# Row tiles on TensorE, transposes and moves on the DMA queues, and a new order, in a fused attention and feed-forward block

## The chip, the core and the metric

The kernel runs on one core of one Trainium2 chip. Time is device microseconds of one execution, the median of several. The profile is one execution on the same core; its span is a little shorter than the time (204.3 us against 206.0 us for the profiled run).

## What is computed

With S = 2048 tokens, D = 448, 16 heads of 28 and F = 1792, all in bfloat16:

```
xn = (x - mean(x)) / sqrt(var(x) + 1e-5)
q, k, v = split(xn @ wqkv)                  # 448 -> 3 x 448
logits[s, w] = q[s] . k[s - 2 w] / sqrt(28) # w = 0..7, positions below 0 masked
o = softmax(logits) @ v                     # over those 8 positions
s = o @ wo
g = silu(gelu(xn @ w1 + b1) @ w2 + b2)
out = x + s * g
```

## The kernel before

Tokens are reordered when they are loaded: the even positions first, then the odd ones (`tok`, `rows`). The dilated window then becomes eight neighbouring tokens. A query block of 120 tokens (the first has 128, `BLK`) needs 128 keys, so all its scores fit in one 128-key tile, and a 0/1 mask on the exponentials (L515) keeps the eight that count. There are 17 blocks, 16 token tiles of 128 and 4 chunks of 512 tokens.

The stages are: statistics and normalisation of a token tile (L317, L318, L344; the standard deviation is a ScalarE square root, L328); a TensorE transpose of the tile and its copy to SBUF (L352, L356); q and k, made already transposed, 112 rows for 4 heads at a time (L374); v, token by token, in the tiles of keys that the blocks want, so 17 tiles (L414); the first feed-forward matmul with the GELU behind it (L442, L447); the second one with bias, tanh and the product for the SiLU (L462, L475, L479, L483); the attention of a block (L503 to L545); and the output projection with the final sums (L555 to L569). The contraction of 448 is cut into 128 + 128 + 128 + 64; the last tile is padded to 128 with zero rows, so it costs a full matmul. For `w1` one of the padding rows holds `b1`, met by a column of ones in xn.

Four heads share 112 partitions of `kT`, so their scores can't be told apart by one matmul of q. The kernel therefore multiplies q by four 0/1 columns (L389, `hm`) into `qx`, four copies in which only one head's rows are not zero, and one matmul (L503) gives four heads of scores, 480 columns. The attention output of a block is transposed on TensorE (L541) and copied (L545) into `oT` for the projection.

The order of the work is not written by hand. Each stage adds tasks to a `_Plan`: an engine, a planned cost, the tasks it depends on, the buffers it takes and gives, and a priority. `_Plan.run` lays the tasks on the engines one by one, the earliest start first and the priority only between equal starts, and the instructions are emitted in that order. On each engine they then run in exactly this order. PSUM is split by purpose: 3 banks for projections and feed-forward, 2 for scores, 1 for the attention output, 2 for transposes. ScalarE works through one chunk's GELUs, then its exponentials, because each needs another table (`gate`).

Of the kernel before, what the change touches and what calls it, by code (L numbers as in the profile page):

```python
# [13 lines left out]
HOP = 0.10  # L14

# [10 lines left out]
class _Task:  # L26
    __slots__ = ("eng", "cost", "deps", "fn", "prio", "take", "give", "slots",
                 "start", "end", "on", "ndep", "users", "tail", "seq")


class _Plan:
# [7 lines left out]
    def add(self, eng, cost, fn, deps=(), prio=0, take=(), give=(), tail=0.0):  # L39
        t = _Task()  # L40
        t.eng = eng if isinstance(eng, tuple) else (eng,)
        t.cost = cost if isinstance(cost, tuple) else (cost,) * len(t.eng)
        t.deps = [d for d in deps if d is not None]
        t.fn, t.prio, t.take, t.give, t.tail = fn, prio, take, give, tail
        t.slots = {}
        t.start = t.end = None
        t.on = None
        t.users = []
        t.seq = len(self.tasks)
        self.tasks.append(t)  # L50
        for p in take:
            if p.fifo is not None:
                p.fifo.append(t)
        return t

    def run(self):
# [4 lines left out]
        free = {}  # L61
        ready = [t for t in self.tasks if not t.ndep]
        order = []
        while ready:
            best = None
            for t in ready:
                slot_at = 0.0
                ok = True
                for p in t.take:
                    if not p.free or p.fifo and p.fifo[0] is not t:  # L70
                        ok = False
                        break
                    slot_at = max(slot_at, min(p.free)[0] + HOP)
                if not ok:
                    continue
                for e, c in zip(t.eng, t.cost):
                    at = max(free.get(e, 0.0), slot_at)
                    for d in t.deps:
                        at = max(at, d.end + (0.03 if d.on == e else HOP))
                    key = (round(max(at, free.get(e, 0.0)), 2) + (c if len(t.eng) > 1 else 0.0) * 0.5,  # L80
                           -t.prio, t.seq)
                    if best is None or key < best[0]:
                        best = (key, t, e, c, at)
            if best is None:
                raise RuntimeError("the plan is stuck: " + str([(t.seq, t.eng, t.fn.__qualname__) for t in ready[:20]]))
            _, t, e, c, at = best
            t.on, t.start = e, at
            free[e] = at + c
            t.end = at + c + t.tail
            for p in t.take:  # L90
                s = min(p.free)
                p.free.remove(s)
                t.slots[id(p)] = s[1]
                if p.fifo is not None:
                    p.fifo.pop(0)
            for p, owner in t.give:
                p.free.append((t.end, owner.slots[id(p)]))
# [11 lines left out]
    def emit(self):  # L109
        done = set()  # L110
        for t in self.order:
# [3 lines left out]
            t.fn(t)  # L115
# [3 lines left out]
def kernel(  # L119
# [12 lines left out]
    nc = tc.nc  # L132
# [6 lines left out]
    KT = 4  # L139
    NMT = F // P  # L140
# [4 lines left out]
    GW = 4 * DH  # L145
# [3 lines left out]
    BLK = [(0, 128, 0)] + [(128 + 120 * i, 120, 120 + 120 * i) for i in range(16)]  # L149
    NB = len(BLK)  # L150
# [17 lines left out]

    x_sb = sb("x_sb", [P, NT, D])
    wqkv = sb("wqkv", [P, KT, 3 * D])  # L170
    w1 = sb("w1", [P, KT, F])
    w2 = sb("w2", [P, NMT, D])
    wo = sb("wo", [P, G, D])
    b2 = sb("b2", [P, D])
    xnT = [sb(f"xnT{c}", [P, KT, CH]) for c in range(NCH)]
    qx = [[sb(f"qx{g}_{c}", [P, 4, CH]) for c in range(2)] for g in range(G)]
    kT = [sb(f"kT{g}", [P, S]) for g in range(G)]
    oT = sb("oT", [P, G, S])
    g2 = [sb(f"g2_{t}", [P, D]) for t in range(NT)]
    ident = sb("ident", [P, P])  # L180
    eps_t = sb("eps_t", [P, 1], F32)
    hm = sb("hm", [P, 4], F32)
    m_gen = sb("m_gen", [P, 4, 120])
    m_b0 = sb("m_b0", [P, 4, 128])
    m_sp = sb("m_sp", [P, 4, 120])
# [7 lines left out]
    p_xn = ring("xn", 3, [P, 512])  # L193
    p_st = ring("st", 4, [P, 6], F32)
    p_q = ring("q", 3, [P, CH])
    p_E = ring("E", 4, [P, 4, P], fifo=True)
    p_rd = ring("rd", 2, [P, H], F32)
    p_os = ring("os", 2, [P, D])
    p_y = ring("y", 2, [P, D], F32)
    p_t = ring("t", 2, [P, D], F32)  # L200
    p_sg = ring("sg", 2, [P, D])
    p_h = ring("h", 19, [P, CH], fifo=True)
    p_v = ring("v", 9, [P, H, 32], fifo=True)
    p_o = ring("o", 3, [P, D])

    def bank(name, shape, dt=F32):
        return psum.tile(shape, dt, name=name)

    p_mm = _Pool([bank(f"mm{i}", [P, 512]) for i in range(3)])
    p_sc = _Pool([bank(f"sc{i}", [P, 4, P]) for i in range(2)], True)  # L210
    p_po = _Pool([bank("po0", [P, H, 32])], True)
    p_tp = _Pool([bank(f"tp{i}", [P, 4, P], BF16) for i in range(2)])
# [3 lines left out]
    def buf(pool, owner):  # L216
        return pool.bufs[owner.slots[id(pool)]]
# [4 lines left out]
    def act(n):  # L222
        return 0.19 + n / 1200.0

    def dve(n, r=1):
        return 0.15 + n / (960.0 * r)

# [6 lines left out]
    POOLC, DVEC = "POOL", "DVE"  # L234
    t_eps = plan.add(DVEC, 0.1, memset("vector", eps_t[:], EPS), prio=99)
    t_pad = []
    for xb in p_xn.bufs:
        a = plan.add(DVEC, 0.1, memset("vector", xb[:, 448:], 0.0), prio=98)
        t_pad.append(plan.add(DVEC, 0.1, memset("vector", xb[:, 448:449], 1.0), [a], prio=98))
# [5 lines left out]
    t_ident = plan.add(POOLC, 0.6, mk_ident, prio=99)  # L245
    t_wz = plan.add(POOLC, 1.2, memset("gpsimd", wqkv[64:, 3, :], 0.0), prio=98)
    t_w1z = plan.add(POOLC, 1.8, memset("gpsimd", w1[64:, 3, :], 0.0), prio=97)

    def mk_hm(_):
        nc.gpsimd.memset(hm[:], 1.0)  # L250
        nc.gpsimd.affine_select(out=hm[:], in_=hm[:], compare_op=ALU.is_ge, fill=0.0, base=0,
                                pattern=[[-DH, 4]], channel_multiplier=1)
        nc.gpsimd.affine_select(out=hm[:], in_=hm[:], compare_op=ALU.is_ge, fill=0.0, base=DH - 1,
                                pattern=[[DH, 4]], channel_multiplier=-1)
    t_hm = plan.add(POOLC, 0.6, mk_hm, prio=96)

    def mk_masks(_):
        for m, n, lo, hi in ((m_gen, 120, -1, 8), (m_b0, 128, 7, 0)):
            nc.gpsimd.memset(m[:], 1.0)
            nc.gpsimd.affine_select(out=m[:], in_=m[:], compare_op=ALU.is_ge, fill=0.0, base=lo,  # L260
                                    pattern=[[0, 4], [-1, n]], channel_multiplier=1)
            nc.gpsimd.affine_select(out=m[:], in_=m[:], compare_op=ALU.is_ge, fill=0.0, base=hi,
                                    pattern=[[0, 4], [1, n]], channel_multiplier=-1)
        q0, n, k0 = BLK[SPLIT]
        j = HALF - q0
        nc.gpsimd.tensor_copy(m_sp[:], m_gen[:])
        nc.gpsimd.affine_select(out=m_sp[:, :, j:], in_=m_sp[:, :, j:], compare_op=ALU.is_ge,
                                fill=0.0, base=k0 - HALF, pattern=[[0, 4], [0, n - j]],
                                channel_multiplier=1)
    t_vw = [plan.add(POOLC, 0.5, memset("gpsimd", v[:], 1.0), prio=80 - i) for i, v in enumerate(p_v.bufs)]  # L270
    t_E = [plan.add(POOLC, 0.5, memset("gpsimd", e[:], 0.0), prio=90) for e in p_E.bufs]
    t_mask = plan.add(POOLC, 5.0, mk_masks, prio=85)

    dma_at = [2.0]

    def dma(eng, dst, src, kb, deps=(), prio=50, give=()):
        def fn(_):
            (nc.sync if eng == "SP" else nc.scalar).dma_start(dst(), src)
        return plan.add(eng, 0.6, fn, deps, prio, give=give, tail=2.0 + kb / 230.0)

    xr = x_sb
    t_x = {}

    def load_x(t0, n, eng, prio, kb):
        d = dma(eng, lambda: xr[:, t0:t0 + n, :],
                rows(x_half, t0 * P, n * P).rearrange("(t p) d -> p t d", p=P), kb, prio=prio)
        for t in range(t0, t0 + n):
            t_x[t] = d

    load_x(0, 1, "SP", 99, 112)  # L290
    load_x(1, 1, "SP", 98, 224)
    load_x(2, 2, "SP", 97, 448)
    t_wqk = [dma("ACT", lambda: wqkv[:, 0:3, 0:2 * D],
                 A_wqkv[0:384, 0:2 * D].rearrange("(k p) c -> p k c", p=P), 900, prio=99),
             dma("ACT", lambda: wqkv[:64, 3, 0:2 * D], A_wqkv[384:448, 0:2 * D], 1000, prio=98),
             t_wz]
    t_wv = [dma("ACT", lambda: wqkv[:, 0:3, 2 * D:],
                A_wqkv[0:384, 2 * D:].rearrange("(k p) c -> p k c", p=P), 1400, prio=97),
            dma("ACT", lambda: wqkv[:64, 3, 2 * D:], A_wqkv[384:448, 2 * D:], 1400, prio=96), t_wz]
    load_x(4, 4, "SP", 96, 1600)  # L300
    load_x(8, 4, "SP", 95, 2000)
    load_x(12, 4, "SP", 94, 2400)
    t_w1 = [dma("SP", lambda: w1[:, 0:3, :], B_w1[0:384, :].rearrange("(k p) c -> p k c", p=P), 3000, prio=93),
# [329 lines left out]
```

The softmax here doesn't subtract the row's maximum and nothing guards it: scores larger than these inputs give would overflow.

## Time and profile before

| | |
|---|---|
| time, median of 3 | 206.07 us (206.0 to 206.94) |
| span of the profiled execution | 204.3 us |
| busy: PE, PEld, DVE, ACT, POOL | 179.2, 96.2, 117.0, 117.2, 14.6 us |
| first projection matmul starts | 12.89 us |
| last output-projection matmuls end | 200.7 us |
| weights, x and outputs moved | 8.80 MB |

PE is TensorE, PEld its weight loads, DVE is VectorE, ACT is ScalarE, POOL is GpSimd, SP is the queue that issues most transfers. The busy time of one matmul is longer than its distance to the next one, because matmuls overlap in the array: the rows of the groups give the first, the chain of work that ended last gives the second. An engine's idle time counts only where the chain passes through it.

### The profile page before, as it was taken

The numbers are of one execution on the slowest core, as the hardware profiler recorded it, in microseconds if no ns is written. First come the engines' busy times: TensorE is split into PE (matmuls) and PEld (weight loads), VectorE is DVE, ScalarE is ACT, GpSimd is POOL, SyncE is SP. The second block draws the span as 40 slices with busy tenths as digits, with TensorE's granted clock in tenths as the row PEclk, the third lists the DMA queues.
The fourth block names the chain that finished last, engine by engine and source line by source line (L and its number), as shares of the span: only waits on it lengthen the run. The fifth ranks groups of instructions, "written<-read, shape, count | busy, mean of one in ns | idle before, by whom it ended". The sixth has DMA issues, their size and how long they took to land.

```text
span 204.3 us, 3123 instructions
## 1 busy us (share of the span) xinstructions
PE 179.2 (88%) x1192; PEld 96.2 (47%) x1192; DVE 117.0 (57%) x330; ACT 117.2 (57%) x204; POOL 14.6 (7%) x32
## 2 busy tenths in 40 slices
PE   0269849989999999989999999899999999799952
PEld 0146324445555644545556544455565544365530
DVE  2795980037987930069977800279976400289992
ACT  0316735786554587766535687855545786856610
POOL 8991000000000000000000000000000000000000
PEclk9999988999999999999999999999999999999995
DMA  6999100000000000000000000000100000000010
GB/s 195 359 369 362 42 0 3 0 0 0 5 22 22 26 0 0 0 0 3 30 16 26 22 0 0 0 3 0 50 22 22 0 0 3 0 0 26 24 45 23
DMA packets 8320, 8.80 MB, mean 43 GB/s; under 512 B 497, under 2 KB 7857, under 8 KB 8306
## 3 DMA queue, kind: packets, MB, share of 16 engines
q1 hardware_dynamic: 7346, 7.40, 11.0%
q10 hardware_dynamic: 960, 1.20, 1.8%
q8 instruction: 9, 0.15, 0.3%
q14 instruction: 5, 0.04, 0.1%
HBM read 6.77 MB, written 1.84 MB: 42 GB/s over the span
## 4 chain that ended last, share of the span: by engine, by line
PE 76%; DVE 13%; ACT 6%; DMA 2%; issue 1%; ACTq 0%; DVEq 0%
PE mm L442 25%; PE mm L462 18%; PE mm L374 13%; PE mm L555 6%; PE sc L503 6%; PE mm L414 4%; PE po L522 3%; DVE st L317 2%; ACT L509 2%; DMA wqkv<-in_A_wqkv_dram 2%; DVE qx L389 2%; DVE E L515 2%; PE tp L541 1%; ACT E L509 1%; DVE xnT L356 1%
## 5 line engine op out<-in xcount | busy, mean ns | idle before, releaser
L442 PE MATMUL mm<-xnT,w 128*128 128x512 bf16 x224 | 51.0, 388 | 0.0
L509 ACT ACTIVATE E<-sc 128x480 bf16<-128x480 f32 (+1 forms) x68 | 36.0, 570 | 23.5 <-PE sc L503 23.2
L462 PE MATMUL mm<-w,h 128*128 128x448 bf16 x224 | 47.6, 352 | 0.0
L447 ACT ACTIVATE h<-mm 128x512 bf16<-128x512 f32 x56 | 32.8, 597 | 13.6 <-PE mm L442 13.1
L442 PEld LDWEIGHTS <-w 128*128 128x128 bf16 x224 | 22.2, 100 | 27.7 <-issue 2.9
L515 DVE TENSOR_TENSOR E<-E,m_gen 128x480 bf16<-128x480 bf16 x60 | 23.1, 402 | 19.1 <-ACT E L509 18.1
L374 PE MATMUL mm<-xnT,wqkv 128*112 128x512 bf16 x128 | 30.4, 391 | 1.0 <-DVE xnT L356 1.0
L462 PEld LDWEIGHTS <-h 128*128 128x128 bf16 x224 | 21.2, 97 | 18.3
L356 DVE COPY xnT<-tp 128x512 bf16<-128x512 bf16 x16 | 6.5, 419 | 38.5 <-PE tp L352 38.5
L374 PEld LDWEIGHTS <-wqkv 128*112 128x112 bf16 x128 | 17.0, 135 | 11.9 <-issue 2.2
L503 PE MATMUL sc<-qx,kT 112*128 112x480 bf16 (+4 forms) x80 | 22.4, 334 | 0.0
L389 DVE TENSOR_SCALAR qx<-q,hm 112x512 bf16<-112x512 bf16 x64 | 18.0, 348 | 6.7 <-ACT q L364 6.7
L522 PE MATMUL po<-v,E 128*128 128x29 bf16 x272 | 17.1, 177 | 4.1 <-DVE E L515 3.9
L522 PEld LDWEIGHTS <-E 128*128 128x128 bf16 x272 | 14.0, 96 | 13.3 <-DVE E L515 8.0
L352 PE MATMUL tp<-ident,xn 128*128 128x128 bf16 x64 | 6.4, 241 | 13.9 <-DVE xn L344 13.9
L555 PE MATMUL mm<-wo,oT 112*128 112x448 bf16 x64 | 15.1, 358 | 0.9 <-DVE oT L545 0.9
L364 ACT CAST q<-mm 112x512 bf16<-112x512 f32 x16 | 9.4, 585 | 10.1 <-PE mm L374 9.5
L479 ACT ACTIVATE t<-y 128x448 f32<-128x448 f32 x16 | 9.2, 577 | 8.8 <-DVE y L475 8.8
L364 ACT CAST kT<-mm 112x512 bf16<-112x512 f32 x16 | 9.4, 586 | 7.2 <-PE mm L374 7.2
L475 DVE TENSOR_TENSOR y<-mm,b 128x448 f32<-128x448 f32 x16 | 10.0, 623 | 3.5 <-PE mm L462 3.5
L352 PEld LDWEIGHTS <-xn 128*128 128x128 bf16 x64 | 4.5, 106 | 15.7 <-DVE xn L344 15.0
L364 ACT CAST v<-mm 128x448 bf16<-128x448 f32 x17 | 9.1, 533 | 5.0 <-PE mm L414 5.0
(49 smaller groups left out, 146.3 us busy)
## 6 DMA issues: line engine op xcount, KB each, us to landing
out_dram<-o SPq DMA_DIRECT2D x16, 112.0 KB, 1.7
w<-in_B_w_dram SPq DMA_DIRECT2D x1, 1568.0 KB, 11.0
x_sb<-in_A_x_dram SPq DMA_DIRECT2D x3, 448.0 KB, 7.9
w<-in_B_w_dram SPq DMA_DIRECT2D x1, 1344.0 KB, 9.5
wqkv<-in_A_wqkv_dram ACTq DMA_DIRECT2D x1, 672.0 KB, 4.4
wo<-in_A_wo_dram SPq DMA_DIRECT2D x1, 392.0 KB, 7.8
wqkv<-in_A_wqkv_dram ACTq DMA_DIRECT2D x1, 336.0 KB, 6.5
x_sb<-in_A_x_dram SPq DMA_DIRECT2D x2, 112.0 KB, 3.6
```

The source lines that it names most:

```text
L352: nc.tensor.transpose(tp[:, kt, :], xn[:, kt * P:(kt + 1) * P], ident[:])
L364: nc.scalar.copy(o, i)
L374: nc.tensor.matmul(ps[:GW, :], wqkv[:, kt, which * D + GW * g:which * D + GW * (g + 1)], xnT[c][:, kt, :], start=(kt == 0), stop=(kt == KT ...
L389: nc.vector.tensor_scalar(qx[g][c % 2][:GW, hl, :], q[:GW, :], hm[:GW, hl:hl + 1], None, op0=ALU.mult)
L442: nc.tensor.matmul(ps[:, :], w1[:, kt, mt * P:(mt + 1) * P], xnT[c][:, kt, :], start=(kt == 0), stop=(kt == KT - 1))
L447: nc.scalar.activation(buf(p_h, _)[:], buf(p_mm, a)[:, :], ACT.Gelu_apprx_tanh)
L462: nc.tensor.matmul(ps[:, :D], buf(p_h, t_h[(c, mt)])[:, j * P:(j + 1) * P], w2[:, mt, :], start=(mt == 0), stop=(mt == NMT - 1))
L503: nc.tensor.matmul(ps[:, :, lo - q0:hi - q0], kT[g][:GW, k0:k0 + P], qx[g][c % 2][:GW, :, lo - c * CH:hi - c * CH], start=True, stop=True)
L509: nc.scalar.activation(buf(p_E, k)[:, :, :nq], buf(p_sc, a)[:, :, :nq], ACT.Exp, scale=SCALE)
L515: nc.vector.tensor_tensor(out=E[:, :, :nq], in0=E[:, :, :nq], in1=m[:, :, :nq], op=ALU.mult)
L522: nc.tensor.matmul(ps[:, h, :DH + 1], E[:, hl, :], buf(p_v, t_v[b])[:, h, :DH + 1], start=True, stop=True)
L555: nc.tensor.matmul(ps[:, :D], oT[:GW, g, t * P:(t + 1) * P], wo[:GW, g, :], start=(g == 0), stop=(g == G - 1))
```

## The change

The change keeps the arithmetic and moves it. Its parts:

- **32-row tiles for the scores.** q and k are now made token by token (`qk_rows`), evacuated with each head padded from 28 to 32 columns, and transposed by DMA into `qkT`, so that a head lies in a 32-partition strip. Sixteen small matmuls of 120 columns make a block's scores, each using 32 rows of the array; four of them, in different strips, write four different banks. The four masked copies of q are no longer needed.
- **64-row pairs for the tails.** The 64-row remainder of the contraction is no longer padded. It lies at partitions 0 to 63 in one half of the tiles and at 64 to 127 in the other, and two tails, one from each half, are issued one after the other (`batch`). Bias `b1` moves into the GELU instruction.
- **DMA instead of engines.** From tile 4 on, xn is transposed by a DMA on the SP queue (`dma_T`), and so are q, k and the attention output. v is computed once per token tile (16 instead of 17) and moved by GpSimd-issued DMAs (`dma_sb`) to the key tiles; the attention output is moved in the same way from blocks of 120 to tiles of 128.
- **The deviation on GpSimd.** (var + eps) to the power -0.5 replaces the square root on ScalarE and a reciprocal on VectorE.
- **Loads in order of use.** x and wqkv come first, in slices by contraction tile, and the first projections follow the slices (`first_batch`); w2 is held back until half of w1 is there, and half of x and wo until later (`hold`). Matmuls on zeros run on TensorE before the data come.
- **One pool of 8 PSUM banks** for everything, and a planner that knows tables, array modes and priorities taken from a list (`PRIO`, `LATER`). The last token tile is worked in two halves of 224 columns. The order of the work is: GELU 0, attention 0 and 1 with the projections of all the later chunks, GELU 1, attention 2, GELU 2, attention 3, GELU 3, each followed by its second feed-forward matmuls.

The core of the diff, with the lines that matter:

```diff
-    p_mm = _Pool([bank(f"mm{i}", [P, 512]) for i in range(3)])
-    p_sc = _Pool([bank(f"sc{i}", [P, 4, P]) for i in range(2)], True)
-    p_po = _Pool([bank("po0", [P, H, 32])], True)
-    p_tp = _Pool([bank(f"tp{i}", [P, 4, P], BF16) for i in range(2)])
+    p_b = _Pool([psum.tile([P, 512], F32, name=f"bank{i}") for i in range(8)])
...
+    def dma_sb(dst, src, deps, prio, take=(), give=()):
+        def fn(k):
+            nc.gpsimd.dma_start(dst(k), src())
...
+    def dma_T(dst, src, deps, prio, give, n=1):
+        def fn(_):
+            nc.sync.dma_start_transpose(out=dst, in_=src())
...
-            nc.scalar.activation(sd[:, t0:t0 + n], mv[:, t0:t0 + n, 1], ACT.Sqrt, bias=eps_t[:])
-            nc.vector.reciprocal(rstd[:, t0:t0 + n], sd[:, t0:t0 + n])
+            nc.gpsimd.tensor_scalar(sd[:, t0:t0 + n], mv[:, t0:t0 + n, 1], eps_t[:], None, op0=ALU.add)
+            nc.gpsimd.tensor_tensor(out=rstd[:, t0:t0 + n], in0=sd[:, t0:t0 + n], in1=half_t[:, :n], op=ALU.pow)
...
+        if t >= TPC:
+            t_xT[t] = dma_T(xnT[:, :, t * P:(t + 1) * P], lambda: buf(p_xn, a)[:], [a], PRIO["turn_x"][t], (p_xn, a, 0))
+            return
...
+    def batch(close, opened, prio):
...
+            todo = [[(j, i) for i, j in enumerate(every) if j.half == h] for h in range(2)]
+            while todo[0] or todo[1]:
+                for h in range(2):
+                    if todo[h]:
+                        j, i = todo[h].pop(0)
...
+        def tail(ps, start, stop):
+            nc.tensor.matmul(ps[:], w1[r, 3, ms], xnT[r, 3, cs], start=start, stop=stop)
...
-                    nc.tensor.matmul(ps[:, :, lo - q0:hi - q0], kT[g][:GW, k0:k0 + P],
-                                     qx[g][c % 2][:GW, :, lo - c * CH:hi - c * CH], start=True, stop=True)
+            for g in range(G):
+                for hl in range(4):
+                    r = slice(32 * hl, 32 * hl + 32)
+                    nc.tensor.matmul(buf(p_b, k, hl)[:, g * nq:(g + 1) * nq], qkT[r, 1, g, k0:k0 + P],
+                                     qkT[r, 0, g, q0:q0 + nq], start=True, stop=True)
...
-                nc.tensor.transpose(tp[:GW, g, :nq], os_[:nq, GW * g:GW * (g + 1)], ident[:nq, :nq])
-            nc.vector.tensor_copy(oT[:GW, :, q0:q0 + nq], buf(p_tp, tr)[:GW, :, :nq])
+            first, d = dma_sb(lambda k, t=t, row=row, n=n: buf(p_ot, ot_at.get(t, k))[row:row + n, :D],
+                          lambda q=q, n=n: buf(p_os, o)[q - q0:q - q0 + n, :], [o] + t_os + mine + [d for _, d in ot[t]],
+                t_oT[t] = dma_T(oT[:, :, t * P:(t + 1) * P], lambda t=t: buf(p_ot, ot_at[t])[:], [d for _, d in ot[t]], PRIO["turn_o"][t],
+                                (p_ot, ot_at[t], 0))
...
+    for c, what in ((0, "F"), (0, "A"), (1, "A"), (1, "F"), (2, "A"), (2, "F"), (3, "A"), (3, "F")):
```

How many instructions of each kind the two kernels hold, on the engines that the change moves:

| | before | after |
|---|---|---|
| first feed-forward, 512 columns | 224 full | 168 full, 56 of 64 rows |
| q and k | 128 of 512 columns | 96 of 448, 32 of 64 rows and 448 |
| v, 448 columns | 68 full | 48 full, 16 of 64 rows |
| scores | 80 (480 columns in most) | 272 of 32 rows and 120 columns |
| attention times v, 29 columns | 272 | 272 |
| transposes on TensorE | 132 | 16 |
| DMA transposes on SP | 0 | 45 |
| GpSimd-issued DMAs | 0 | 67 |
| ScalarE table loads | 9 | 8 |
| changes of the array's tile size in TensorE's order | 0 | 72 |

## The prediction

> **What bounds the kernel now.** I read the shares of busy time and the 40 slices first, to see whether one engine is busy throughout.
>
> ```profile
> PE 179.2 (88%) x1192; PEld 96.2 (47%) x1192; DVE 117.0 (57%) x330; ACT 117.2 (57%) x204; POOL 14.6 (7%) x32
> ...
> PE   0269849989999999989999999899999999799952
> PEld 0146324445555644545556544455565544365530
> DVE  2795980037987930069977800279976400289992
> ```
>
> PE is full from the fourth slice to the last but two, with holes at the start, near slices 5 and 6, and at the end. VectorE comes in bursts of up to 9 tenths, so it is close behind PE in the attention stages. The chain that ended last says the same: 76% of the span on PE.
>
> ```profile
> PE 76%; DVE 13%; ACT 6%; DMA 2%; issue 1%; ACTq 0%; DVEq 0%
> ```
>
> So time is won by taking columns off PE, or by closing holes. To price PE I need the distance between matmuls, not their busy time (388 ns for 512 columns holds some of the neighbour's time too). The chain in order of time gives it:
>
> ```profile
> 73.48 12.25 PE mm L442 x56
> ...
> 68.41 4.32 PE mm L374 x20
> ...
> 95.67 0.21 PE sc L503
> ...
> 95.89 0.76 PE mm L555 x4
> ...
> 96.84 1.33 PE mm L462 x7
> 98.17 0.21 PE tp L541 x4
> 98.38 0.09 PE po L522 x4
> ```
>
> A matmul of 512 columns takes 12.25/56 = 0.218 us (L374: 0.216), one of 448 columns 1.33/7 = 0.190, four transposes 0.21, a score matmul 0.21, four small matmuls of 29 columns with their four weight loads 0.09.
>
> Before, PE's sum is then: L442 224 x 0.218 = 48.8; L462 32 x 1.33 = 42.6; L374 128 x 0.216 = 27.6; L414 68 x 0.190 = 12.9; L555 16 x 0.77 = 12.3; scores 68 x 0.21 = 14.3; L522 68 x 0.09 = 6.1; transposes of x and of the attention output 33 x 0.21 = 6.9. Together 171.5. The first projection starts at 12.89 and the last matmuls end at 200.7, which is 187.8 us; so some 16 us in between are holes, 12.9 is the start and 3.6 the tail. The windows show the first hole and the end:
>
> ```profile
> 25.00:29.00 4.00, 0.48 (x6) 0.36 (x7) 3.84 (x14) 1.06 (x3) 0.00 (x0) 1.00 0.00 0
> 29.00:43.00 14.00, 14.00 (x65) 6.23 (x64) 1.10 (x6) 8.85 (x15) 0.00 (x0) 0.88 0.00 1
> ...
> 174.00:200.70 26.70, 22.93 (x201) 12.66 (x199) 20.20 (x51) 14.21 (x26) 0.00 (x0) 0.98 0.06 18
> ```
>
> Columns: length, then busy time of PE, PEld, DVE, ACT, POOL, then granted clock. From 25 to 29 us PE waits while VectorE does statistics (3.5 us lost), and after it the clock is 0.88 for 14 us (1.6 lost). In the last 27 us PE loses nearly 4, because the last attention blocks run through VectorE with no other matmuls left to fill in.
>
> **What the Trainium skill says.** TensorEngine Tiling (Array Packing), Key Properties: tiles of the array work independently and in parallel, and changing the tile size drains the array. No run so far shows either; what the trace gives is the pipeline that a drain would empty, 388 - 218 = 170 ns. TensorE: Matmul & The Clock Gate, Measured speedup vs the span model: four 32-row tiles with 512 columns ran 3.07 times faster than one by one; not shown here. DMA: Bandwidth & Descriptors, Latency and other measured facts: a DMA has some 2 us of fixed cost, and a transposing one moved 261 GB/s; the trace agrees with the first (112 KB stores land 1.7 us after issue) and has no transpose. SBUF - State Buffer, the "DVE blocks DMA" trap: GpSimd can't write the descriptors of its own DMAs while VectorE runs a two-port operation; no such DMA is in this trace.
>
> **The change on PE.** Tails in pairs: 168 full matmuls and 28 pairs in place of 224, (168 + 28) x 0.218 = 42.7, 6.1 less than before. Second feed-forward matmul: unchanged, 42.6. q and k: (96 + 16) x 0.190 = 21.3, 6.3 less. v: (48 + 8) x 0.190 = 10.6, 2.3 less. Output projection 12.3 and attention times v 6.1, unchanged. Transposes: two of the four that remain come after the first projection, 0.4; 6.5 less. All this counts a pair as one matmul.
>
> Scores: 16 small matmuls in a block. If four stream side by side, 120/512 of 0.218 x 16/4 = 0.20 us; one by one 0.82; the nearest row is L522, where 16 small matmuls with 16 weight loads take 4 x 0.09 = 0.36. I take 0.37, as the weight loads are of the same width: 17 x 0.37 = 6.3, 8.0 less than before. (Ends: 3.4 and 13.9.)
>
> Added: 72 changes of tile size, 19 groups of tails and 17 of scores, each entered and left. One costs between 0 and the 0.17 us of the pipeline; I take the middle, 0.085: 6.1. (Ends: 0 and 12.2.)
>
> PE's sum after: 42.7 + 42.6 + 21.3 + 10.6 + 12.3 + 6.1 + 0.4 + 6.3 + 6.1 = 148.4, 23 less than before.
>
> **The start.** Before, the first matmul waits for all four tiles of the chunk, for a table load behind ACT's own transfers (to 6.98) and the order of VectorE's work. After, tile 0 alone starts it: its statistics end at 4.3 in the trace, then two tiny GpSimd operations (0.11 to 0.2 each in the rows of small GpSimd work; 0.5 with the hops), xn 0.47 and its tail's copy (0.15), transposes and copy about 1.1: 6.6 us. The wqkv slices (1.2 MB behind 0.45 MB of x, at the 360 GB/s of the early slices) are there by 4.6 + 2. So 6.3 us come off. The first half of w1 follows by about 10 us, before it is wanted at about 15 (6.6 + 42 x 0.19), and statistics of later tiles run under the first GELUs, when VectorE had almost nothing to do: the hole at 25 us and the slow clock behind it should go.
>
> **Holes.** Of the 16 us before, 5 go with that hole, and about 4 at the end, since the last attention blocks now come ahead of the last GELUs; 7 stay. New waits: a block's scores want four banks at once, freed by four exponentials of 0.57 in a row, with the next blocks of PE's order queued behind them; q and k pass a DMA (2 + 0.26 MB/261 GB/s = 3.0 us by the page's prices) before the scores, the attention output two of them (about 2 + 2.5) before the projection. PE's order has other matmuls between, so most of it is hidden; I add 3, with 0 and 15 as ends.
>
> **The other engines.** ScalarE: exponentials 38.7, GELUs 33.4, tanh 9.4, 34 copies of 0.53 (18.1), 8 tables of 1.28: 110. VectorE: masks 27.3, statistics 12.5, y, g and sg 30, normalised outputs and reciprocals 14.7, xn 8.6, 15 evacuations 9.3, o and the rest 8: 111. Both stay under 148. The tightest place is between the first and the second group of GELUs: by the new order PE has about 34 us there, ScalarE 32 exponentials, 4 tanh, 17 copies and a table, 31, and VectorE 8 blocks of 2.5, 4 tiles of y and g (5.0), statistics of 4 tiles (3.1), xn of 8 (4.2) and 5 evacuations (3.1), 35, part of which can slip under the next GELUs. Removed from VectorE are L389 (18.0), L356 and L545 (10) but evacuations and late statistics come into the same stretch; this is why I leave 3 us of new holes and not 0. SP: 45 transposes and 17 stores; at 3.0, 2.5 and 1.7 us with no overlap at all 16 x 3.0 + 28 x 2.5 + 17 x 1.7 = 147. GpSimd: 61 moves of about 1 us, off the path. Both are hidden if those prices hold.
>
> **Sum.** Start 6.6 + PE 148.4 + holes 10 + tail 3.4 (half-size last pieces) = 168.4; the time lies 1.7 above the span before, so 170. I give 169, since the drains and the score loads may partly overlap.
>
> **Rivals.** (a) Tiles don't run side by side and every drain costs the full pipeline. Then tails cost 28 x 0.218 + 24 x 0.190 = 10.7 more, scores 17 x 0.45 = 7.6, drains 6.1: 193, still faster. For it: nothing in the trace shows two matmuls in parallel. Against: L522 takes 23 ns for each pair of load and matmul, so issue is no obstacle. (b) A wait takes the place of columns: banks, or q, k and attention output coming late out of their DMA, 3 to 4 us in each of four attention stages, about 14: 183. For it: the chain of a block gets two or three DMA trips longer, and the tight stretch above. Against: the blocks of other chunks lie between. (c) The queue becomes the bound: if each transpose holds SP for twice the price, one after the other, 16 x 6 + 28 x 5 + 29 = 265 us of queue, and even with a third of it overlapped the end is at about 215, slower than before. For it: all 45 stand in one queue, in a fixed order, each holding up those behind it. Against: a fixed cost that is mostly latency overlaps with the next transfer, as the stores' and loads' do here.
>
> **Chances.** 68% for the sum (160 to 178), 9% for (a), 16% for (b), 6% for (c), 1% for no change. Faster by more than 0.5%: 0.93; same 0.01; slower 0.06. The range must hold the sum and (b), and leaves (a) and (c) out: low end with free drains, 0.2 us of scores and no new holes (169 - 6 - 3 - 3, and a little for pairs), 158; high end 184.
>
> **What would show it.** In the profile after: pairs of tails 0.22 us apart in the chain, not 0.44; a block's 16 scores in about 0.4 us; first L498 matmul near 6.6 us; no PE hole at 25 us, clock near 1 from the start; PE's share of the chain above 85%; SP transposes landing in 2 to 4 us. I am wrong if the waits of PE name DMA tiles (qkT, oT, v) or banks for more than 10 us in all, if tails don't pair, or if transposes queue behind each other.

## The result and the profile after

The median of four runs is 171.19 us (170.53 to 172.78), against 206.07 us (206.0 to 206.94) for the kernel before in the same runs: a ratio of 0.831, 95% interval 0.823 to 0.839. Here and below, an execution over 1.5% above the fastest one of its kernel counts as slow and is left out of times and ratios, though the traces of tails_one_half and plain_priorities are of such executions. The forecast was 169 us in a range of 158 to 184. The profiled execution took 172.78 us, the longest of the four; its span is 171.1 us, 33.2 less than before.

The page of the kernel after gives busy time, the slices that answer to those shown of before, and the granted clock. A slice is 4.3 us here.

```profile
PE 156.6 (92%) x1313; PEld 77.4 (45%) x1313; DVE 101.9 (60%) x271; ACT 102.7 (60%) x183; POOL 52.1 (30%) x114
...
PE   7999999904999999999999999999999999999950
PEld 2644344402454564334445454335555545445640
DVE  4778530039489988965047888004988994605770
...
PEclk9999999975599999999999999999999999999998
```

PE is full nearly from the second slice to the end, except for one hole in slices 9 and 10, and the clock drops to 0.5 behind it. The chain that ended last has only 72% on PE and 15% on transfers:

```profile
PE 72%; DMA 15%; issue 3%; DVE 3%; POOL 3%; SPq 0%; DVEq 0%; POOLq 0%
```

Some pieces of this chain in order of time give the distances between matmuls (start, length, count):

```profile
98.47 0.32 PE bank L636 x16
98.80 0.20 PE bank L658 x4
...
138.60 2.59 PE bank L557 x12
141.19 0.97 PE bank L560 x8
142.16 2.70 PE bank L557 x12
144.86 0.79 PE bank L658 x32
...
148.46 1.43 PE bank L593 x7
```

L557 is a full matmul of 512 columns, still 2.59/12 = 0.216 us. L560 are eight tails of 64 rows: 0.97 us is four times 0.218 and 0.10 for the change of tile size, so two tails cost as much as one full matmul. The group behind them takes 2.70 in place of 2.59, which is the change back, 0.11. A block's scores (L636) take 0.32 us in the chain; with the same 0.10 for the change, 0.22 are left for the columns. The four small matmuls of L658 behind them take 0.20 in place of 0.09, again the change back.

The windows of the kernel after, in the columns of the prediction's windows, cut the span where PE's state changes:

```profile
7.66:34.10 26.44, 26.33 (x174) 11.72 (x172) 11.61 (x35) 16.68 (x28) 11.48 (x21) 1.00 1.08 229
34.10:40.80 6.70, 0.01 (x2) 0.01 (x1) 3.80 (x11) 0.71 (x2) 1.62 (x4) 0.69 0.66 207
40.80:48.00 7.20, 7.20 (x39) 3.07 (x39) 4.69 (x12) 4.02 (x9) 1.48 (x2) 0.57 0.29 57
48.00:164.10 116.10, 116.10 (x1060) 58.67 (x1059) 75.45 (x185) 79.62 (x144) 30.72 (x56) 1.00 0.52 95
```

So the span is: start 7.66, first stretch 26.4, a hole of 6.7, a stretch of 7.2 at 0.57 of the clock (3.1 lost), 116 us in which PE never waits, and a tail of 7.0. PE's own work is 164.07 - 7.66 - 6.7 - 3.1 = 146.6 us, against the 171.5 summed up for before.

What made the hole stands in the waits from 12 to 41 us of the same trace:

```profile
DVE st L391 <- DMA x_sb<-in_A_x_dram: 14.3, 2, 13.6
...
PE bank L658 <- DVE E L650: 6.7, 1, 6.7
...
POOL x_sb L739 <- DMA xnT<-xn: 3.9, 1, 3.9
```

PE waited for the masked exponentials of the first block, but they were late only because VectorE, which works in a fixed order, had stood for 13.6 us on the statistics of tile 8. Its x had not been asked for: GpSimd issued that load at 32.14, after `hold` (L739) had waited for the transposed tile 7. And tile 7 stood in the SP queue behind the transposes of q and k, which the timeline of SP shows (start, length, engine, line, operation):

```profile
13.82 15.05 SPq L351 DMA_TRANSPOSE qkT<-qk_tok  x4
28.96 15.59 SPq L351 DMA_TRANSPOSE xnT<-xn  x5
```

Four transposes took 15 us to issue, while w2 (1568 KB) was moving from 13.66 to 26.8; most later ones took 1.2 to 1.3 us each. That the load is what slowed them isn't shown by a run of its own. Tile 7 is the first of the five x transposes, issued at 28.96, and the hold could run at 31.59.

### The profile page after: what moved, and what is told of

The parts are those of the page before. It is cut to its first block, busy times and chain, and to the rows that moved or that the text cites. A ratio compares the mean times of both kernels' runs of the same rounds, so it can differ in the third digit from the quotient of the medians.

```text
span 171.1 us, 3569 instructions
## 1 busy us (share of the span) xinstructions
PE 156.6 (92%) x1313; PEld 77.4 (45%) x1313; DVE 101.9 (60%) x271; ACT 102.7 (60%) x183; POOL 52.1 (30%) x114
## 4 chain that ended last, share of the span: by engine, by line
PE 72%; DMA 15%; issue 3%; DVE 3%; POOL 3%; SPq 0%; DVEq 0%; POOLq 0%
PE bank L593 22%; PE bank L557 16%; DMA w<-in_B_w_dram 12%; PE bank L498 10%; PE bank L700 7%; PE bank L658 4%; PE bank L524 4%; PE bank L560 3%; PE bank L636 3%; DMA x_sb<-in_A_x_dram 3%; PE bank L501 2%; DVE st L391 1%; PE bank L527 1%; DVE y L609 1%; DVE sg L705 0%
## 5 line engine op out<-in xcount | busy, mean ns | idle before, releaser
L593 PE MATMUL bank<-w,h 128*128 128x448 bf16 (+1 forms) x238 | 46.5, 342 | 0.0
L564 ACT ACTIVATE h<-bank,b 128x512 bf16<-128x512 f32 x56 | 34.2, 692 | 12.5 <-PE bank L560 6.5
L557 PE MATMUL bank<-xnT,w 128*128 128x512 bf16 x168 | 39.1, 379 | 0.0
L642 ACT ACTIVATE E<-bank 128x480 bf16<-128x480 f32 (+1 forms) x68 | 33.3, 581 | 9.6 <-PE bank L636 9.4
L345 POOL DMA_DIRECT2D ot<-os x31 | 16.8, 545 | 52.7 <-DVE os L670 38.1
L345 POOL DMA_DIRECT2D v<-v_tok x30 | 16.3, 549 | 29.2 <-ACT v_tok L303 18.0
L557 PEld LDWEIGHTS <-w 128*128 128x128 bf16 x168 | 15.5, 98 | 20.7 <-issue 3.8
L498 PE MATMUL bank<-w_in,xnT 128*128 128x448 bf16 x96 | 24.5, 380 | 0.1
L658 PEld LDWEIGHTS <-E 128*128 128x128 bf16 x272 | 11.3, 97 | 13.1 <-DVE E L650 7.1
L700 PE MATMUL bank<-wo,oT 128*128 128x448 bf16 (+1 forms) x68 | 14.7, 341 | 0.0
L524 PE MATMUL bank<-w_in,xnT 128*128 128x448 bf16 x48 | 12.1, 352 | 0.0
L670 DVE TENSOR_TENSOR os<-bank,rd 120x448 bf16<-120x448 f32 (+1 forms) x17 | 10.6, 622 | 0.5
L658 PE MATMUL bank<-v,E 128*128 128x29 bf16 x240 | 10.7, 176 | 0.0
```

The lines of the kernel that those rows point to most:

```text
L345: nc.gpsimd.dma_start(dst(k), src())
L498: nc.tensor.matmul(ps[:, :D], xnT[:, kt, cs], w_in[:, kt, which * D:(which + 1) * D], start=start, stop=stop)
L524: nc.tensor.matmul(ps[:, :D], xnT[:, kt, k0:k0 + P], w_in[:, kt, 2 * D:], start=start, stop=stop)
L557: nc.tensor.matmul(ps[:], w1[:, kt, ms], xnT[:, kt, cs], start=start, stop=stop)
L564: nc.scalar.activation(buf(p_h, own, i)[:], buf(p_b, own, i)[:], ACT.Gelu_apprx_tanh, bias=b1[:, mt:mt + 1])
L593: nc.tensor.matmul(ps[:, :n], buf(*h_at[(c, mt)])[:, j * P:(j + 1) * P], w2[:, mt, cs], start=(mt == 0), stop=(mt == NMT - 1))
```

## Experiments

Each ratio is to runs of the kernel before taken with it; in microseconds of that kernel, 0.01 is 2.1 us. All but two kernels are edits of the kernel after (171.19 us, 0.831). The first five try the theory of the hole and the two kinds of tiles.

**x_early** issues the load of x 8 to 15 right behind w2 and b2, without the hold. `move` takes tasks out of the finished order and puts them behind another.

```diff
     load_x(12, 4, 85, "POOL", [t_hold])
+    held = t_hold
...
     plan.run()
...
+    issues = [t_x[8].deps[0], t_x[12].deps[0]]
+    held.fn = None
+    for t in issues:
+        t.deps = []
+    move(issues, t_b2.deps[0])
```

> The changed kernel with one edit: the loads of x tiles 8 to 15 are issued right behind w2 and b2 and no longer wait for the last turned tile of chunk 1; all other orders stay. Mine: the hole of 6.7 us on TensorE at 34 us is a queue on VectorE, statistics of tile 8 that wait for this load ahead of the first masks. x then lands near 31 in place of 36.8 us, the hole shrinks to under 2 us, the clock stays at 1, and the time falls by 5 to 8 us, to about 164. Rival: the DMA engines are simply full until 40 us, so the earlier load pushes w2 and the turned tiles back by as much and the hole only moves: within 1.5 us of 171.

Measured: 164.13 us, ratio 0.794 (0.789 to 0.799), as I expected. The clock is 0.99 and PE's largest hole 1.4 us, a wait for a transposed tile of x:

```profile
PE bank L498 <- DMA xnT<-xn: 1.4, 1, 1.4
```

It follows that the held load was the cause: the hole of 6.7 us and the slow clock went. The only other thing that moved is the load of wo, which stood behind the same hold and goes out at 26.20 in place of 33.69 us; its first user, L700, runs long after the hole.

**stats_later** leaves the load as it is and moves VectorE's statistics of tiles 8 to 11 behind the masks and sums of the first block.

```diff
+    dve = [t for t in plan.order if t.on == "DVE"]
+    xn8 = next(t for t in dve[dve.index(t_st[11]):] if t.fn.__qualname__.endswith("norm.<locals>.f1"))
+    move([t_st[t] for t in range(8, 12)] + [t_rs[8]], dve[dve.index(xn8) - 1])
```

> The changed kernel with one edit: on VectorE the statistics of tiles 8 to 11 stand behind the first block's masks and the first y and g, not ahead of them; loads are untouched. Mine: the masks run at 33 us, attention times v follows at once and the hole of 6.7 us at 34 us goes by at least half, though xn of tile 8 still waits for its x and holds up the masks of the second block; 3 to 6 us less. Rival: TensorE waits for loads whatever VectorE's order, so the hole stays and the time is within 1.5 us of 171.

Measured: 169.26 us, 0.818 (0.814 to 0.823), 1.9 us less and not the 3 to 6 that I expected. The old wait went, and a new one of 4.2 us came later on PE, with a slow clock behind it:

```profile
PE bank L636 <- DVE os L670: 4.2, 1, 4.2
```

The scores wait here for a bank that VectorE frees only after the statistics and xn of tile 8, which still begin at 36.60 us, when x has landed. So VectorE's order hands the wait on, but most of the late load still has to be paid.

**tails_one_half** puts all first feed-forward tails into the lower half of the array, with the order untouched.

```diff
-        r = slice(64 * half, 64 * half + 64)
+        r = slice(0, 64)
```

> The changed kernel with one edit: all 56 tails of the first feed-forward matmul use partitions 0 to 63, so no two of them can lie side by side; same order, same number of instructions. Mine: pairs do run side by side, so 28 pairs of 0.218 us become 56 in a row: 6.1 us slower, 177. Rival: tails run one after the other already, each with its own columns: no change.

Measured: 175.08 us, 0.848 (0.844 to 0.853). In the chain, eight tails take twice the columns:

```profile
143.89 1.83 PE bank L560 x8
```

1.83 - 0.97 = 0.86, or 0.215 for each of the four tails that no longer find a partner. All 28 pairs make 6.0 us on PE. Of this 4.2 us show between the spans (175.3 and 171.1 us) and 3.9 between the medians: chunk 0's seven pairs, 1.5 us, fall ahead of the hole, which is 1.2 us shorter in this trace (5.5 us). The pairs do run side by side.

**scores_by_strip** makes the scores strip after strip, so that neighbours in PE's order share a strip.

```diff
-            for g in range(G):
-                for hl in range(4):
+            for hl in range(4):
+                for g in range(G):
```

> The changed kernel with one edit: a block's 16 score matmuls are issued strip by strip (four in one 32-row strip, then the next strip) and not strip after strip in turn. Mine: overlap needs neighbours in different strips, so most of the side-by-side work is lost: a block's scores take 0.6 to 0.8 us in place of 0.22 and the 17 blocks 6 to 10 us more, near 179. Rival: matmuls of other strips overtake, and the time stays at 171 with scores at 0.2 us.

Measured: 173.34 us, 0.840 (0.837 to 0.844), an interval that overlaps that of the kernel after. A block's scores take 0.35 us in place of 0.32:

```profile
48.70 0.35 PE bank L636 x16
```

In this trace the hole is 8.1 us long, 1.4 more, so the 2.1 us between the medians can't be put down to the scores. My expectation was wrong and the rival's right about the size: neighbours in the same strip cost next to nothing. That a matmul waiting for its strip lets those of other strips pass is one explanation, and no run shows it. It was left open whether strips matter at all:

**scores_one_strip** takes every head's q and k from the first strip, so the scores of the other heads are replaced by those of the first in each group of four.

```diff
-                    r = slice(32 * hl, 32 * hl + 32)
+                    r = slice(0, 32)
```

> The changed kernel with one edit: all 16 score matmuls of a block read the first 32-row strip, so the three other heads of each group get the first one's scores; the output is not the reference's. Instructions, columns and order are the same. Mine: here nothing can lie side by side, so a block's scores take 16 x 120 columns at 2.4 a ns, 0.8 us in place of 0.22 to 0.32, and 17 blocks 8 to 10 us more, near 180; the run by strips was quick because matmuls of the next strip start while the last is still streaming. Rival: a small matmul costs its issue of about 14 ns whatever its strip, and the side-by-side tiles gained nothing: 171 to 173.

Measured: 181.68 us, 0.876 (0.868 to 0.885), 10.5 us more by the medians. The chain has every block at

```profile
48.16 0.94 PE bank L636 x16
```

Without the change of tile size this is 0.84 against 0.22, a factor of 3.8 for four strips; 17 blocks times 0.62 us are 10.5. So strips run side by side.

**x8_early** follows from x_early, whose two loads shared the DMA engines with w2: only tiles 8 to 11 go early, 12 to 15 stay held.

```diff
-    t_hold = hold(x_sb[:1, 8:NT, 0], xnT[:1, 0, 8 * P - 1:8 * P].to_broadcast((1, 8)), [t_xT[7]], 180)
+    t_hold = hold(x_sb[:1, 12:NT, 0], xnT[:1, 0, 8 * P - 1:8 * P].to_broadcast((1, 4)), [t_xT[7]], 180)
...
+    issues = [t_x[8].deps[0]]
+    for t in issues:
+        t.deps = []
+    move(issues, t_b2.deps[0])
```

> The changed kernel with x tiles 8 to 11 alone loaded behind w2; tiles 12 to 15 stay held as in the changed kernel. x_early kept a hole of 1.4 us at 34 us, where TensorE waits for the turned tile 4, which stands behind four transposes that share the DMA engines with w2 and 0.9 MB of x. Mine: with 0.45 MB less in that stretch the turned tile lands 1 us or more sooner and the hole goes: about 163. Rival: the queue of transposes sets it and the time is x_early's, 164.

Measured: 162.92 us, 0.787 (0.783 to 0.790), the fastest version, 8.3 us below the change as it was made. The interval just touches x_early's, so the times hardly tell these two apart; the traces do. The page of x8_early shows no hole at all:

```profile
PE   6999999999999999999999999999999999999940
```

PE works from 7.76 to 154.3 without a stop, so its sum is 146.5 us, the same as was found above by taking the hole and the slow clock out.

**turn_x_first** is x_early with the transposes of q and k of tiles 2 and 3 put behind that of x tile 7 on SP. It was meant to bring x tiles 4 to 7 ahead of them.

```diff
+    move([t_qk[2].deps[0], t_qk[3].deps[0], t_qk[2], t_qk[3]], t_xT[7].deps[0])
```

> The kernel of x_early with one edit: on SP the transposes of x tiles 4 to 7 stand ahead of those of q and k of tiles 2 and 3, which are wanted later. Mine: the turned tile 4 is there before 30 us, the hole of 1.4 us at 34 us goes, but q and k of tile 2 may now be late for the third block of attention; 0.5 to 1.5 us faster than x_early, near 163. Rival: the array waits for q and k of tile 2 or 3 in place of it, and it is the same or up to 3 us slower.

Measured: 163.93 us, 0.791 (0.786 to 0.796), not to be told from x_early; the hole is 0.9 in place of 1.4 us. But the edit didn't do what it was meant to do. Tile 7 stands first among the x transposes, so only that one came ahead:

```profile
13.43 10.16 SPq L351 DMA_TRANSPOSE qkT<-qk_tok  x2
26.56 1.19 SPq L351 DMA_TRANSPOSE xnT<-xn  x1
27.85 4.36 SPq L351 DMA_TRANSPOSE qkT<-qk_tok  x2
32.30 6.01 SPq L351 DMA_TRANSPOSE xnT<-xn  x4
```

PE goes on at 34.80, 2.5 us after the issue at 32.30, which is what these transposes take to land: it waited for the second one, still behind q and k. So whether this order is what keeps the hole of x_early open is not decided by this run.

**no_warm** is x_early without the matmuls on zeros ahead of the first data.

```diff
+    for t in plan.tasks:
+        if t.prio == -1:
+            t.fn = None
```

> The kernel of x_early with one edit: the 31 matmuls on zeros ahead of the first data are not issued. In the kernel before, without them, the first 16 projection matmuls took 4.92 us, 0.31 each in place of 0.216, so the array seems to start slow. Mine: the first 16 to 25 projection matmuls take 0.3 to 0.4 us again and the time grows by 1 to 3 us over x_early's 164.3. Rival: the early matmuls wait for weights and copies anyway and nothing is lost: within 1 us.

Measured: 165.24 us, 0.799 (0.794 to 0.805); the interval overlaps that of x_early, so the 1.1 us between the medians isn't sure. The chains show the effect on PE plainly. In no_warm the first projections run at half rate for about 3 us:

```profile
8.59 0.37 PE bank L524
8.96 0.75 PE bank L498 x2
```

In x_early, with the zeros:

```profile
8.77 0.19 PE bank L524
8.96 0.38 PE bank L498 x2
```

In no_warm the first 15 projections are done at 12.21 us, in x_early at 10.66, so about 1.5 us of PE time are lost; half of it comes back, since the hole at the later wait is 0.6 us in place of 1.4.

**plain_priorities** keeps all parts and drops the searched lists: every stage's priorities fall evenly.

```diff
+    PRIO = {k: tuple(100 - 80 * i / len(v) for i in range(len(v))) for k, v in PRIO.items()}
+    LATER = {k: 30 for k in LATER}
```

> The changed kernel with all priorities of the plan replaced by ones that fall evenly from the first tile to the last, and one offset for all later steps: every part of the change but the searched order. Mine: TensorE's columns are the same, so only holes differ: 5 to 15 us more holes than the 9 of the changed kernel, 176 to 186, still well below 206. Rival: the searched order is most of the gain and it comes out near 195 or above; or it is worth nothing, and it is at 171.

Measured: 189.43 us, 0.916 (0.908 to 0.925), more than the 176 to 186 that I expected and less than the rival's 195. PE's waits are now spread over masked exponentials (5.1 us), exponentials (1.7), a transposed attention output (3.7) and a moved v (2.6), and two stretches run at half clock. About half of the gain hangs on the order: some 17 us come from the parts with this plain order, and 18 more from the listed one. Another plain order could divide it otherwise.

**root_on_scalar** puts the deviation back on ScalarE and VectorE, as before the change.

```diff
+            nc.scalar.activation(sd[:, t0:t0 + n], mv[:, t0:t0 + n, 1], ACT.Sqrt, bias=eps_t[:])
...
-            nc.gpsimd.tensor_scalar(sd[:, t0:t0 + n], mv[:, t0:t0 + n, 1], eps_t[:], None, op0=ALU.add)
-            nc.gpsimd.tensor_tensor(out=rstd[:, t0:t0 + n], in0=sd[:, t0:t0 + n], in1=half_t[:, :n], op=ALU.pow)
...
+            nc.vector.reciprocal(rstd[:, t0:t0 + n], sd[:, t0:t0 + n])
```

> The changed kernel with the deviation as before: square root on ScalarE (with its table) and reciprocal on VectorE, in place of the two GpSimd operations; the plan then lays the order anew. ScalarE gains 3 table loads of 1.28 us in mid-kernel and 7 short operations. Mine: start a little quicker, as 0.9 us of GpSimd operations ahead of the first xn become about 0.5, but tables break into the exponentials: 1 to 4 us slower, 172 to 175. Rival: ScalarE has slack everywhere and nothing changes, or it is faster because GpSimd's operations hold up its own moves.

Measured: 178.36 us, 0.866 (0.857 to 0.876), 7 us more than the kernel after and not the 1 to 4 that I expected. The planner laid the whole order anew around 11 table loads, and PE waits for q and k (3.7 us) and masks (4.9). So this is the price of that other order as much as of the square root, and the experiment doesn't tell them apart. The next but one asks in the other direction.

**before_b2_gpsimd** asks why the tail became longer. It is the kernel before, with b2's load issued by GpSimd.

```diff
-    t_b2 = dma("SP", lambda: b2[:], b2_src.to_broadcast((P, D)), 4800, prio=89)
+    t_b2 = plan.add("POOL", 0.6, lambda _: nc.gpsimd.dma_start(b2[:], b2_src.to_broadcast((P, D))), prio=10, tail=20.0)
```

> The kernel before with one edit: b2 is loaded by a DMA issued from GpSimd and not from SP. Mine: what lies between the last VectorE operation and the end of the span, 2.5 us in the kernel before and 4.8 us in the changed one and in its variants, grows as soon as one transfer is issued from GpSimd, whose end has more to wait for; so about 2.2 us slower, 208.3, with the last VectorE operation where it was. Rival: the 2.2 us come from the two small stores at the end or from transposes, and this stays at 206.1.

Measured: 207.08 us, 1.000 (0.998 to 1.003): no change where I expected 2.2 us more, so a GpSimd-issued transfer alone doesn't lengthen the end.

**before_pow_gpsimd** is the kernel before with the deviation on GpSimd, and nothing else changed.

```diff
-            nc.scalar.activation(sd[:, t0:t0 + n], mv[:, t0:t0 + n, 1], ACT.Sqrt, bias=eps_t[:])
-            nc.vector.reciprocal(rstd[:, t0:t0 + n], sd[:, t0:t0 + n])
+            nc.gpsimd.tensor_scalar(sd[:, t0:t0 + n], mv[:, t0:t0 + n, 1], eps_t[:], None, op0=ALU.add)
+            nc.gpsimd.tensor_tensor(out=rstd[:, t0:t0 + n], in0=sd[:, t0:t0 + n], in1=half_t[:, :n], op=ALU.pow)
```

> The kernel before with one part of the change alone: the deviation as an add and a power on GpSimd, in place of ScalarE's square root and VectorE's reciprocal. Mine: within -1.5 to +2 us of the kernel before. ScalarE saves a table load of 1.28 us ahead of the first chunk, but GpSimd is busy with memsets and masks until about 12 us, so the later deviations of the first chunk come no sooner; and the time from the last VectorE operation to the end of the span stays near 2.6 us. Rival 1: the start comes 1 to 2 us earlier, and the time is 204 to 205. Rival 2: the power on GpSimd is what makes the end of the program longer after the change: the time from the last VectorE operation to the end grows from 2.6 to near 4.8 us.

Measured: 205.23 us, a ratio of 0.992 (0.990 to 0.995), which is about 1.6 us. Rival 1 was nearest: the first projection starts at 11.30 in place of 12.89, and the span is 1.5 us shorter. The later deviations did wait behind GpSimd's masks, as I had thought, but v's projection of the first tiles could start without them. From the last VectorE operation to the end it is still 2.6 us, so the power isn't what lengthens the tail either.

**The tail, from the traces.** What the two kernels of before couldn't show, the instructions at the end of all these traces do. At the end of each trace every engine has drain instructions and exchanges semaphores with the others. In the kernel after, GpSimd's drains are (count, shortest/median/longest in ns, first and last start in us):

```profile
L862 POOLq DRAIN  x3: 46/106/6782, 163.5 to 170.8; - x3
```

The long one, 6.78 us, begins at 163.5 with GpSimd's last operation, the final sum of tile 14 (L710, 163.52 to 164.70), and ends at 170.3, 0.8 ahead of the end of the span; the last semaphore instructions of TensorE, ScalarE and VectorE begin only then, at 170.4. VectorE was done at 166.31. In plain_priorities that sum fell to VectorE, and GpSimd's last work is a transfer issued at 163.65:

```profile
L864 POOLq DRAIN  x3: 46/102/6117, 163.6 to 189.3; - x3
```

There the drain is over by 169.8, long before the end at 189.6, and the last VectorE operation is 2.6 us from the end, as before the change. The nine other edits of the kernel after all have GpSimd's sum at the end, a drain of 6.78 or 6.79 us, and an end 4.7 to 4.8 us after VectorE. In the kernel before, where GpSimd issues no transfer, the drain ends with GpSimd's last memset (15.9 us); in before_b2_gpsimd it ends 4.8 us after the issue, but at 21.3 us, where nobody waits. All these traces fit one reading: in a kernel that issues transfers on GpSimd, a GpSimd operation this late costs about 2.2 us at the end. It is read from the traces and not shown by an experiment, since taking only that sum off GpSimd wasn't tried. What GpSimd does in the 5.6 us after its last operation stays open.

## Why the prediction was right, and where its steps were off

**Columns.** PE's sum was forecast at 148.4 and measured at 146.6; the last eight half-size matmuls of the output projection run in the tail and would add 0.76 at the chain's price. Pairs at 0.22 us, and the unchanged rates of full matmuls, came out as worked. This agrees with what the Trainium skill says under TensorEngine Tiling (Array Packing), Key Properties: tiles work in parallel. Rival (a) falls with tails_one_half and scores_one_strip: only where no two matmuls can lie side by side do they cost what they cost one by one, 0.215 us a tail and 0.84 us a block (0.218 and 0.82 in the prediction).

**Scores.** Mis-sized: 0.37 us a block forecast, 0.22 measured, so 17 blocks cost 3.7 in place of 6.3. The nearest row, L522 with a weight load for each small matmul, was too slow a guide; the estimate of four full streams, 0.20, was nearer. The Trainium skill (TensorE: Matmul & The Clock Gate, Measured speedup vs the span model) has a factor of 3.07 for four tiles of 512 columns; at 120 columns it is 3.8 here.

**Changes of tile size.** The middle of the two ends, 0.085, was close: 0.10 to 0.11, so 72 changes cost 7.2 to 7.9 in place of 6.1.

**Start.** 6.6 forecast, 7.66 measured. The largest part that was off is the two GpSimd operations, taken as 0.5 us with their hops from rows of smaller work. The add waited 0.33 for a mask in GpSimd's own queue, and then took 0.31, and the power 0.58; from the statistics to xn it is 1.34 us. The start is still 5.2 earlier than before. before_pow_gpsimd has 1.6 of that from the deviation alone. The rest presumably comes from starting on tile 0 and slices of the weights; no run tries these alone.

**Holes.** 10 us forecast, 6.7 + 3.1 = 9.8 measured, and this agreement is luck. I expected seven scattered old ones and three new ones. None of the old ones is left, nor that at the end, and x8_early shows that PE needn't stop once. All 9.8 belong to one wait that I had not named: the load of x 8 to 15, held behind a transpose behind other transposes. My claims that there would be no early hole and that the clock would be near 1 from the start were wrong between 34 and 48 us. I had the hold in front of me, and priced transfers from issue to landing, but didn't ask when the issue itself would come, and what in VectorE's queue stands behind the instruction that waits for it.

**Rival (b)** was right in kind and small in size: a wait on a transfer took the place of columns, once, for 9.8 us in all, and through a load and not through q, k or the attention output, whose waits on PE are 0.

**Rival (c)**, the SP queue as the bound of the whole kernel, is refuted: most transposes hold the queue for 1.2 to 1.3 us, and all 45 together for some 70 us and not 236. But what it named, transposes that hold up those behind them, did happen at 14 to 29 us and is a link in the chain that made the hole; it is also one of the signs of being wrong that the prediction listed. Landing, forecast at 2 to 4 us, has medians of 2.5 (x), 3.5 (attention output) and 4.6 (q and k), but up to 14.1 next to the load of w2, where the forecast failed.

**Other engines.** DVE 102 and ACT 103 were forecast at 111 and 110. Both lie under PE. GpSimd's 61 moves took about 0.55 us each to issue, and PE waited for none of them, so the trap with VectorE that the prediction names left no mark on the time; no run tries it by itself.

**Chain.** Above 85% on PE was forecast, 72% came. PE was as busy as forecast; but the chain goes back from the hole through the load of x, GpSimd's queue and the loads of w1 and w2, past 26 us in which PE worked without setting the end.

**Tail.** Mis-sized: 3.4 forecast, 7.0 measured. Six half-size VectorE operations follow the last feed-forward matmul in place of two whole ones (2.2 us in place of 1.05), and what lies between the last VectorE operation and the end, where GpSimd's drain is, grew by 2.2.

**Sums.** Two figures of the prediction don't follow from their working: the low end of the range, 169 - 6 - 3 - 3, is 157 at most and not 158, and in rival (c) two thirds of 265 us of queue are 177, which doesn't lead to 215 us.

In sum: PE 1.8 less, start 1.1 more, holes 0.2 less, tail 3.6 more; 168.4 becomes 171.1. That is the longest of the four executions; where the median one is 1.6 us shorter isn't known. No run puts the transposes back on TensorE, or the loads back in their old order, alone: what these parts bring is known from PE's sum and from the start only.

## What to carry to other kernels

Short contractions that fill half or a quarter of the array are worth pairing, at some 0.1 us for each change of tile size, if they are gathered into groups. When work moves to DMA queues, follow each load back to what allows its issue: a held load behind a queue of transposes can stop an engine that has nothing to do with either. Near the end of a program look at the closing drain too; keeping a late operation off an engine that has issued transfers is worth a try.

## What was not expected of the hardware

- Score matmuls of one strip issued in a row cost next to nothing (0.35 us a block against 0.32): the order within this group of tiles hardly mattered, as long as the group used all strips.
- After a hole of 6.7 us PE's clock was at 0.57 on average for 7.2 us, and without the zeros ahead of the data the first projections ran at half rate for 3 us. The Trainium skill describes both (TensorE: Matmul & The Clock Gate, Part 1: The HAM clock gate): idle time halves the clock until work has gone on for a while. A hole of 4.2 us in stats_later had the same effect, holes of 0.9 and 1.4 us had none.
- Four SBUF to SBUF transposes took 15 us to issue beside a load of 1568 KB.
